# A second order for the first chunk of an attention and softplus-FFN kernel: 582 tasks re-sorted over five engines, 66 of them on another engine

## The chip, the core and the metric

The kernel runs on one core of a Trainium2 chip. The core has a matrix engine (TensorE, PE in the profile), a vector engine (VectorE, DVE), an activation engine (ScalarE, ACT), a general engine (GpSimd, POOL) and a sync engine (SyncE, SP) that here only issues transfers. The metric is the device time of one execution in microseconds (us); lower is better.

## What is computed

Eight batches, eight heads, 576 positions, head width 64. Four heads attend to the last 32 positions, four to the positions at the same place in every 32. Then each token's 512 numbers go through a 512 to 2048 product, a softplus, and a 2048 to 512 product.

```python
scores = scale * np.matmul(q, k.transpose(0, 1, 3, 2))
scores = np.where(masks[None, :, :, :], scores, -1000000000.0)
attn = np.exp(scores - np.max(scores, axis=-1, keepdims=True))
attn = attn / (np.sum(attn, axis=-1, keepdims=True) + 1e-09)
x = np.matmul(attn, v).transpose(0, 2, 1, 3).reshape(B * S, H * D)   # 4608 x 512
h = x @ w_in                                                          # 512 x 2048, float64 weights
g = np.maximum(h, 0.0) + np.log1p(np.exp(-np.abs(h)))
out = g @ w_out                                                       # 2048 x 512, float64 weights
```

## The kernel before, in words

Work is cut twice. Attention goes by *queries* n = 0 to 31, each one batch and one pair of heads; four queries make a batch. The FFN goes by *chunks* of 512 tokens, nine in all, and each chunk by 16 *blocks* f of 128 hidden units. For a block, `hidden` (line 648, 12 matmuls of 512 columns, three for each of four pairs) makes `ph`; ScalarE takes |h|, exp and log (lines 660, 663, 665); VectorE joins them into the softplus `u` (line 669); `u` is split into a high and a low part `gh` and `gl` (lines 264 and 681); `output` (line 688, 12 matmuls) adds the block's share to the four `py` banks. `ph` has two buffers, so block f+2 in the order waits for the softplus of block f.

During the first chunk everything else happens besides: the first eight queries are worked, and all 32 blocks of weights arrive as 64-bit floats (`load_weights`, lines 569 and 575) and are turned into two 32-bit parts each by six steps: `w_abs` (line 589, ScalarE), `w_shift` (line 593), `w_last` (line 602), `w_sign` (line 619, all three VectorE), `w_high` (line 264, a cast) and `w_low` (line 634, a subtraction). A query has its own steps: load q, lay q out (line 264, letter D), load k, scores (S, line 355), maxima (X, line 389), bias (x, line 393) or subtraction, exponentials (E), row sums' guard and reciprocal (r, line 439, and R, line 443), normalising (M, line 447), transposes (T and C on TensorE and a copier for queries 0 to 3; P, line 457, 16 VectorE transposes for queries 4 to 7), the weighted sum (V, line 525) and the two parts of x (H, line 563, and L, line 561).

The order of this first part is not computed. It is the string `FIRST`, a list of task names that is gone through from left to right; each task issues its instructions on its engine's queue, and each engine works its queue strictly in order. A name is a letter for the step and a number for the query or block: `S40` is the first half of the scores of query 4, `F3` the hidden product of block 3, `O3` its output product, `li3` the low part of the input weights of block 3. `Fa0` is the first nine matmuls of block 0 and `F0` the last three; `Q..` are the same steps for the first two blocks of chunk 1. Three further lists, `ON_POOL`, `ON_VECTOR` and `ON_SCALAR`, name the tasks that run on another engine than their usual one: GpSimd's usual tasks are the low parts (`li`, `lo`, `Gl`) and M, VectorE's are r and x, ScalarE's are D, C and the casts (`hi`, `ho`, `Gh`).

Loads are issued on SP's queue, also in order. A load of a query waits there for the buffer that it overwrites (`prob`, `v_in`, `kT`), and everything behind it waits too. The results of chunk 0 (`y0` to `y3`, line 704) are stored from the same queue.

After `FIRST`, a planner (`Plan`) orders the rest from costs and due times. Its first step is the scores of query 8, `S8`, which needs `k8`, the last task but a few of `FIRST`.

Of the kernel before, what the change touches and what calls it, by code (L numbers as in the profile page):

```python
# [33 lines left out]


FIRST = """
q0 D00 k0 W mask D01 S01 q1 X01 x01 D11 q2 D10 S00 X00 Y00 E01 D20 E00 Z00 r0 D21 R0 M0 k1 S10 X10
S11 wi2 ai2 X11 Y11 E11 T00 wi4 k2 S20 ai4 Bi2 x10 E10 di2 k3 ci2 Bi4 Z11 hi2 di4 r1 ci4 T01 C01
C00 q3 D30 D31 T02 X20 R1 Y20 M1 v0 V00 C02 H00 wi1 E20 ai1 S21 X21 L00 Z20 T10 wi0 li2 x21 T11
hi4 Bi1 di1 ci1 E21 r2 V01 H01 L01 C11 wo0 S31 C10 R2 v1 hi1 S30 X30 wo14 li4 wo1 T12 Y30 ai0 X31  # L40
M2 V10 H10 L10 T21 k4 C12 Bi0 v2 wi3 x31 E30 di0 Z30 V11 C21 E31 H11 T20 C20 li1 L11 ao1 T22 r3 R3
M3 V20 T32 ao0 ci0 C22 Bo0 H20 L20 C32 hi0 ai3 T30 C30 do0 wo3 li0 T31 V21 v3 co0 C31 V31 H21 L21
ho0 V30 Bi3 di3 ao3 H30 Fa0 Bo3 ci3 hi3 H31 L30 wi10 q4 D4 L31 F0 lo0 A0 Fa1 do3 co3 li3 Ae0 ho3
Al0 Bo1 do1 u0 S40 X40 wo4 ao4 lo3 Bo4 wo2 ao2 x40 Bo2 Gh0 Gl0 wi8 ai8 wo9 wi6 Bi8 E40 F1 F3 A3
Ae3 do2 di8 ci8 hi8 Al3 co2 do4 co1 ho1 wo5 A1 Ae1 Al1 u3 li8 Gh3 O0 lo1 ho2 lo2 ai6 u1 wi5 ai5
S41 wi11 X41 x41 Gl3 Bi5 Gh1 Gl1 ai11 Bi11 Bi6 E41 F4 wo7 q5 D5 wi9 wi15 F2 A2 di5 O1 di11 Ae2 Al2
di6 ci5 r4 hi5 ci6 wi14 R4 wi12 ci11 hi11 k5 wi13 u2 Gh2 M4 S50 X50 F8 co4 x50 P4 Gl2 O2 li11 A4
Ae4 hi6 ho4 li5 li6 Al4 u4 E50 S51 X51 v4 V40 ai9 Bi9 di9 x51 A8 wo6 Ae8 Al8 wi7 k6 q6 lo4 wo11
ao5 Bo5 O3 ci9 ai7 Bi7 di7 u8 Gh4 Gl4 F5 H40 L40 E51 ci7 ai10 Bi10 r5 R5 F6 Gh8 do5 D6 S60 hi7
di10 Gl8 co5 M5 V41 ci10 A5 Ae5 Al5 u5 O4 li7 A6 Ae6 Al6 X60 x60 u6 ho5 P5 Gh5 Gl5 hi9 lo5 wo12  # L50
li9 F7 H41 hi10 ao7 li10 v5 O5 ao6 Bo6 do6 L41 co6 E60 S61 X61 Gh6 Gl6 A7 Ae7 Al7 x61 Bo7 k7 V50
u7 F9 ho6 lo6 O6 wo10 H50 L50 ai13 Bi13 wo8 ao8 E61 q7 V51 Bo8 D7 di13 do7 A9 Ae9 ci13 r6 R6 hi13
S70 do8 li13 F13 co8 H51 co7 M6 Al9 u9 Gh7 ao10 X70 x70 L51 ho8 Gl7 F10 P6 ho7 ai12 lo7 Gh9 Gl9
lo8 E70 Bi12 Bo10 O7 ao9 Bo9 do10 S71 v6 V60 do9 k9 O8 co9 ho9 A13 Ae13 Al13 u13 F11 di12 A10 Ae10
Al10 Gh13 X71 u10 ao11 Bo11 co10 ho10 lo9 lo10 Gh10 Gl10 x71 H60 L60 do11 ai14 Bi14 O9 A11 V61
ci12 di14 E71 r7 R7 O10 hi12 ai15 ci14 Ae11 li12 H61 L61 co11 hi14 M7 li14 wo15 Al11 u11 F12 P7
Gh11 Gl11 wo13 ao12 A12 Ae12 F14 ho11 lo11 Gl13 ao13 Al12 u12 Gh12 A14 Ae14 Bo12 do12 Gl12 co12
ho12 O11 Bi15 di15 lo12 ci15 ao15 Bo15 v7 V70 H70 L70 ao14 Bo14 Qa0 Al14 u14 O12 q8 D8 hi15 li15
Bo13 do13 co13 ho13 lo13 do14 co14 ho14 V71 H71 F15 A15 Ae15 L71 O13 Q0 Gh14 Gl14 lo14 O14 Al15
u15 Gh15 Gl15 Q1 v8 do15 co15 ho15 lo15 QA0 Qu0 QA1 O15 y0 Qh0 k8 Ob15 Ql0 y3 y2 Qu1 Qh1 Ql1 y1 q9  # L60
"""

ON_POOL = """
x01 D10 D20 hi2 D30 hi0 hi3 ho1 x50 hi6 Gh8 x60 hi13 x70 ho9 Gh13 x71 ho11 hi15 ho14 Gh15 ho15
""".split()
ON_VECTOR = """
D00 M1 C21 M3 li0 lo0 li3 Gl0 li8 Gh3 lo1 Gl3 Gl1 lo4 Gl8 M5 Gl6 li13 lo9 lo10 Gl10 li12 M7 Gl12
lo12 li15 lo13 Gh14 Gl14 lo14 Gl15 lo15
""".split()
ON_SCALAR = """  # L70
y3
""".split()

WIDE = """
# [945 lines left out]
```

## Time and profile before

| | us |
|---|---|
| median of 3 runs | 899.62 |
| lowest and highest run | 898.74, 899.64 |
| the profiled execution's own time | 898.62 |
| its span, first to last instruction | 896.8 |
| TensorE busy in the span | 878.9 |
| VectorE, ScalarE, GpSimd busy | 601.3, 446.8, 58.1 |

The span leaves out 1.8 us of the execution (898.62 less 896.8). TensorE is busy in 98% of the span, so at most 17.9 us can be won by closing its gaps; the matmuls themselves are the same before and after. TensorE's granted clock is 0.999 in this profile. In the views below, a row of the timeline gives start, duration, engine and line, and in brackets the idle time ahead of it with what ended it; a row of the groups gives count, busy time and the mean duration in ns; a row of the stretches gives busy time of PE, PEld (weight loads), DVE, ACT and POOL in turn.

### The profile page before, as it was taken

The numbers are of one execution on the slowest core, as the hardware profiler recorded it, in microseconds if no ns is written. First come the engines' busy times: TensorE is split into PE (matmuls) and PEld (weight loads), VectorE is DVE, ScalarE is ACT, GpSimd is POOL, SyncE is SP. The second block draws the span as 40 slices with busy tenths as digits, with TensorE's granted clock in tenths as the row PEclk, the third lists the DMA queues.
The fourth block names the chain that finished last, engine by engine and source line by source line (L and its number), as shares of the span: only waits on it lengthen the run. The fifth ranks groups of instructions, "written<-read, shape, count | busy, mean of one in ns | idle before, by whom it ended". The sixth has DMA issues, their size and how long they took to land.

```text
span 896.8 us, 14347 instructions
## 1 busy us (share of the span) xinstructions
PE 878.9 (98%) x5632; PEld 722.0 (81%) x5632; DVE 601.3 (67%) x1313; ACT 446.8 (50%) x795; POOL 58.1 (6%) x81
## 2 busy tenths in 40 slices
PE   6899999999999999999999999999999999999998
PEld 4777777888888888888888888888888888888886
DVE  8999996877777677666766676776776333333332
ACT  7998765445444545544544444454443343333332
POOL 6244330000000000000000000000000000000000
PEclk9999999999999999999999999999999999999999
DMA  9882212112211112111211121111200010001001
GB/s 339 297 303 92 86 37 88 44 57 60 76 43 45 44 44 89 32 44 45 91 44 44 42 76 31 44 45 44 91 18 18 1 48 1 0 1 48 1 1 47
DMA packets 50083, 58.27 MB, mean 65 GB/s; under 512 B 3168, under 2 KB 35296, under 8 KB 50016
## 3 DMA queue, kind: packets, MB, share of 16 engines
q1 hardware_dynamic: 49728, 57.03, 19.5%
q8 instruction: 44, 0.72, 0.3%
q10 hardware_dynamic: 288, 0.33, 0.1%
q14 instruction: 23, 0.19, 0.1%
HBM read 47.91 MB, written 9.44 MB: 64 GB/s over the span
## 4 chain that ended last, share of the span: by engine, by line
PE 87%; DVE 8%; ACT 2%; issue 1%; POOL 1%; DMA 0%; SPq 0%; DVEq 0%; POOLq 0%; ACTq 0%
PE py L688 41%; PE ph L648 40%; PE ps L355 2%; PE pv L525 2%; DVE pt L457 2%; PE po L525 1%; PE po L355 1%; DVE a_i L602 1%; DVE a_i L619 1%; DVE a_i L593 1%; DVE u L669 1%; DVE a_o L602 1%; DVE st L389 1%; DVE a_o L619 0%; DMA kT<-in_qk_dram 0%
## 5 line engine op out<-in xcount | busy, mean ns | idle before, releaser
L688 PE MATMUL py<-w_o,gh 128*128 128x512 f32 x1152 | 359.2, 393 | 0.3 <-POOL w_o L634 0.2
L648 PE MATMUL ph<-x_h,w_i 128*128 128x512 f32 x1152 | 356.4, 391 | 1.3 <-DVE w_i L634 0.9
L660 ACT ACTIVATE u<-ph 128x512 f32<-128x512 f32 x144 | 86.2, 599 | 396.8 <-PE ph L648 394.7
L648 PEld LDWEIGHTS ph<-x_h,w_i 128*128 128x128 f32 x1152 | 215.6, 188 | 47.2 <-DVE w_i L634 1.2
L688 PEld LDWEIGHTS py<-w_o,gh 128*128 128x128 f32 x1152 | 214.1, 188 | 47.7 <-POOL w_o L634 1.1
L648 PE MATMUL ph<-x_l,w_i 128*128 128x512 f32 x576 | 224.4, 390 | 0.0
L688 PE MATMUL py<-w_o,gl 128*128 128x512 f32 x576 | 224.4, 390 | 0.0
L669 DVE SCALAR_TENSOR_TENSOR u<-ph,u 128x512 f32<-128x512 f32 x144 | 99.2, 689 | 169.5 <-ACT u L665 167.9
L457 DVE STREAM_TRANSPOSE pt<-prob 32x192 f32<-32x192 f32 x448 | 137.1, 314 | 6.4
L688 PEld LDWEIGHTS py<-w_o,gl 128*128 128x128 f32 x576 | 108.2, 188 | 22.6
L648 PEld LDWEIGHTS ph<-x_l,w_i 128*128 128x128 f32 x576 | 108.2, 188 | 22.5
L681 DVE TENSOR_TENSOR gl<-u,gh 128x512 fp32r<-128x512 f32 x137 | 94.8, 692 | 12.0 <-POOL gh L264 0.8
L663 ACT ACTIVATE u<-u 128x512 f32<-128x512 f32 x144 | 91.2, 633 | 4.5
L665 ACT ACTIVATE u<-u 128x512 f32<-128x512 f32 x144 | 91.0, 632 | 4.3
L264 ACT COPY qT<-prob 64x576 f32<-64x576 f32 x56 | 70.6, 1261 | 2.3 <-DMA prob<-in_qk_dram 1.9
L264 DVE CAST gh<-u 128x512 fp32r<-128x512 f32 x130 | 55.7, 428 | 10.6 <-DVE u L669 0.5
L416 DVE TENSOR_TENSOR prob<-ps,mask_b 128x384 f32<-128x384 f32 x24 | 13.4, 558 | 50.2 <-PE ps L355 50.2
L355 PEld LDWEIGHTS ps<-kT,qT 128*64 128x64 f32 x720 | 24.0, 138 | 9.6 <-issue 8.1
L355 PE MATMUL ps<-kT,qT 128*64 128x64 f32 x720 | 27.6, 225 | 0.9 <-DMA kT<-in_qk_dram 0.9
L525 PE MATMUL pv<-pt,v_in 128*64 128x96 f32 x396 | 22.1, 248 | 1.0 <-PE ps L355 1.0
L447 DVE TENSOR_TENSOR prob<-prob,st 128x576 f32<-128x576 f32 x27 | 21.6, 799 | 0.9
L416 DVE TENSOR_TENSOR prob<-po,mask_b 128x192 f32<-128x192 f32 x24 | 8.6, 357 | 19.3 <-ACT x_h L563 19.3
(101 smaller groups left out, 511.9 us busy)
## 6 DMA issues: line engine op xcount, KB each, us to landing
v_in<-in_v_dram SPq DMA_DIRECT2D x28, 320.0 KB, 3.5
out_dram<-o SPq DMA_DIRECT2D x35, 256.0 KB, 2.1
ri<-in_moe_w_in_dram SPq DMA_DIRECT2D x16, 512.0 KB, 8.0
ro<-in_moe_w_out_dram SPq DMA_DIRECT2D x16, 512.0 KB, 6.9
kT<-in_qk_dram SPq DMA_DIRECT2D x28, 288.0 KB, 2.9
prob<-in_qk_dram SPq DMA_DIRECT2D x28, 288.0 KB, 2.7
v_in<-in_v_dram SPq DMA_DIRECT2D x28, 48.0 KB, 2.7
room<-in_v_dram SPq DMA_DIRECT2D x4, 320.0 KB, 6.8
```

Of the source, the lines that this page charges most:

```text
L264: (engine.copy if engine is nc.scalar else engine.tensor_copy)(dst, src)
L355: nc.tensor.matmul(ps[rows[place], 64 * (x - lo) : 64 * (x - lo) + 64], lhsT=blocks_of(n)[:, c // 32].rearrange("p h l -> p (h l)"), rhs=k ...
L416: nc.vector.tensor_tensor(pv, sv, m, op=ALU.add)
L457: nc.vector.transpose(pt[32 * (i + c) : 32 * (i + c) + 32, h, a : a + hi - lo, 32 * i : 32 * i + 32,], src[:, lo:hi, 32 * c : 32 * c + 32],)
L525: nc.tensor.matmul(po[64 * h : 64 * h + 64, TILE * x : TILE * x + TILE], lhsT=vs[n][:, a, h, :], rhs=pt_of(n, a)[:, h, a % 2], start=True, ...
L648: nc.tensor.matmul(ph, lhsT=w32["i", f][:, half, cc * P : (cc + 1) * P], rhs=x_of(x, cc)[:, t0 : t0 + n], start=(i == 0), stop=(i == 3 * N ...
L660: nc.scalar.activation(us[c, f], phs[c, f], AF.Abs)
L663: nc.scalar.activation(u, u, AF.Exp, scale=-1.0)
L665: nc.scalar.activation(u, u, AF.Ln, bias=1.0)
L669: nc.vector.scalar_tensor_tensor(u, in0=phs.pop((c, f)), scalar=0.0, in1=u, op0=ALU.max, op1=ALU.add)
L681: engine.tensor_tensor(g, us.pop((c, f)), ghs[c, f].bitcast(F32), op=ALU.subtract)
L688: nc.tensor.matmul(py[t], lhsT=g[:, sl], rhs=w32["o", f][:, half], start=(f == 0 and n == 0), stop=(f == NFC - 1 and n == 2),)
```

## The change

`FIRST` is replaced by another list of the same names; no task is added or dropped, and `Plan` is not touched. Of the three engine lists, `ON_POOL` grows from 22 names to 36, `ON_VECTOR` goes from 32 to 31, `ON_SCALAR` keeps one name (`y1` for `y3`). The table, cut to its first lines and its end:

```diff
 FIRST = """
-q0 D00 k0 W mask D01 S01 q1 X01 x01 D11 q2 D10 S00 X00 Y00 E01 D20 E00 Z00 r0 D21 R0 M0 k1 S10 X10
+W mask q0 D01 D00 k0 S01 q1 D10 D11 k1 S00 X01 x01 E01 S11 X00 Y00 X11 Y11 E00 q2 D20 Z00 S10 X10
...
-Bo13 do13 co13 ho13 lo13 do14 co14 ho14 V71 H71 F15 A15 Ae15 L71 O13 Q0 Gh14 Gl14 lo14 O14 Al15
-u15 Gh15 Gl15 Q1 v8 do15 co15 ho15 lo15 QA0 Qu0 QA1 O15 y0 Qh0 k8 Ob15 Ql0 y3 y2 Qu1 Qh1 Ql1 y1 q9
+ho15 u15 Gh15 Gl15 O14 lo15 Qu0 Qh0 Ql0 Q1 QA1 Ob15 Qu1 O15 k8 y1 y0 y2 Qh1 Ql1 y3
 """
 
 ON_POOL = """
-x01 D10 D20 hi2 D30 hi0 hi3 ho1 x50 hi6 Gh8 x60 hi13 x70 ho9 Gh13 x71 ho11 hi15 ho14 Gh15 ho15
+D11 x01 D20 r0 x10 hi1 x21 r1 hi8 x31 r3 hi2 hi6 hi5 hi3 x41 ho1 r4 x50 ho3 x51 r5 x60 ho7 hi7 Gh8
+r6 Gh10 x71 hi14 r7 Gh13 ho12 hi15 ho14 ho15
 """.split()
 ON_VECTOR = """
-D00 M1 C21 M3 li0 lo0 li3 Gl0 li8 Gh3 lo1 Gl3 Gl1 lo4 Gl8 M5 Gl6 li13 lo9 lo10 Gl10 li12 M7 Gl12
-lo12 li15 lo13 Gh14 Gl14 lo14 Gl15 lo15
+D00 M0 li1 M3 C22 li6 Gh0 Gl0 li5 li3 lo1 Gl2 Gh5 Gl5 li9 Gl9 lo5 Gl6 lo6 Gl8 M6 li12 lo10 li14
+li15 Gl13 Gh14 Gl14 lo14 Gh15 lo15
 """.split()
```

Counted over these lists, GpSimd gains 4 biases (x), 7 guards (r), 4 casts, one weight low part, one `Gl` and one M, and loses one D. VectorE loses those biases and guards, one low part, one `Gl` and one M, and gains two casts of `Gh`: its queue has 12 rows fewer. ScalarE loses casts and gains one D. Line numbers after the edit are one higher throughout, since the string has one line more.

**GpSimd at the start.** The rows that follow the last clearing memset; `st` is the small table of maxima, sums and reciprocals of a query, `raw_q` a loaded q, `early_l` and `early_h` the buffers of queries 0 to 3. Before:

```order
L393 TENSOR_SCALAR st_0_175<-st_0_175 128x3
L264 COPY early_h2_92<-raw_q1_173 64x18x32
L264 COPY early_h1_94<-raw_q2_179 64x18x32
L447 TENSOR_TENSOR early_l0_91<-early_l0_91,st_0_175 128x9x64
L264 CAST w_i_2_283<-a_i_2_235 128x512
L264 COPY early_h3_96<-raw_q3_301 64x18x32
L634 TENSOR_TENSOR w_i_2_283<-a_i_2_235,w_i_2_283 128x512
```

And now, from the same place:

```order
L265 COPY early_h2_92<-raw_q1_173 64x32x18
L394 TENSOR_SCALAR st_0_192<-st_0_192 128x3
L265 COPY early_h1_94<-raw_q2_212 64x18x32
L440 TENSOR_SCALAR st_0_192<-st_0_192 128x9
L394 TENSOR_SCALAR st_1_208<-st_1_208 128x6
L265 CAST w_i_1_265<-a_i_1_236 128x512
L394 TENSOR_SCALAR st_2_275<-st_2_275 128x3
L440 TENSOR_SCALAR st_1_208<-st_1_208 128x9
L448 TENSOR_TENSOR early_l2_93<-early_l2_93,st_1_208 128x9x64
```

The first bias (`x01`, the `128x3` row) now stands behind a copy of q, the guards have come in from VectorE, and the first normalising (`M0`) has gone to VectorE, with that of query 1 (`M1`) here in its place.

**TensorE at the first blocks.** `ph_0_0` and `ph_0_1` are blocks 0 and 1, `ps_4_0` the scores `S40` of query 4 with their mask. From the last matmuls of block 0, before:

```order
L648 MATMUL ph_0_0_617<-x_l3_632,w_i_0_551 128x512
L648 MATMUL ph_0_1_646<-x_h0_331,w_i_1_409 128x512 x2
L648 MATMUL ph_0_1_646<-x_l0_347,w_i_1_409 128x512
L648 MATMUL ph_0_1_646<-x_h2_455,w_i_1_409 128x512 x2
L648 MATMUL ph_0_1_646<-x_l2_457,w_i_1_409 128x512
L648 MATMUL ph_0_1_646<-x_h1_546,w_i_1_409 128x512 x2
L648 MATMUL ph_0_1_646<-x_l1_548,w_i_1_409 128x512
L340 LDWEIGHTS ident_b_108
L340 MATMUL ps_4_0_666<-mask_b_89,ident_b_108 64x384
```

Now:

```order
L649 MATMUL ph_0_0_625<-x_l3_617,w_i_0_507 128x512
L341 LDWEIGHTS ident_b_108
L341 MATMUL ps_4_0_654<-mask_b_89,ident_b_108 64x384
L341 LDWEIGHTS ident_b_108
L341 MATMUL ps_4_0_654<-mask_b_89,ident_b_108 64x384
L356 MATMUL ps_4_0_654<-kT_0_100,qT_99 64x64 x12
L649 MATMUL ph_0_1_685<-x_h0_331,w_i_1_265 128x512 x2
```

The scores of query 4 now stand directly behind block 0; the nine matmuls of `Fa1` that lay between come after them.

**SP at the end of the chunk.** `v_in` is the load of `v8`, `kT_0` that of `k8`, `out_0_dram` the stores of chunk 0. Before:

```order
L293 DMA v_in_102<-in_v_dram 96x128
L300 DMA v_in_102<-in_v_dram 128x5x128
L704 DMA out_0_dram<-o_0_0_1778 128x512
L282 DMA kT_0_100<-in_qk_dram 128x576
L704 DMA out_0_dram<-o_0_3_1792 128x512
```

Now:

```order
L294 DMA v_in_102<-in_v_dram 96x128
L301 DMA v_in_102<-in_v_dram 128x5x128
L283 DMA kT_0_100<-in_qk_dram 128x576
L705 DMA out_0_dram<-o_0_1_1791 128x512
L705 DMA out_0_dram<-o_0_0_1794 128x512
```

The load of `k8` has moved past the first store, ahead of all four.

More of the change, by code (lines that the diff above doesn't have):

```diff
@@ L36 @@
 FIRST = """
-q0 D00 k0 W mask D01 S01 q1 X01 x01 D11 q2 D10 S00 X00 Y00 E01 D20 E00 Z00 r0 D21 R0 M0 k1 S10 X10
[L38 to L58, printed above, removed]
-Bo13 do13 co13 ho13 lo13 do14 co14 ho14 V71 H71 F15 A15 Ae15 L71 O13 Q0 Gh14 Gl14 lo14 O14 Al15
@@ L60 @@
-u15 Gh15 Gl15 Q1 v8 do15 co15 ho15 lo15 QA0 Qu0 QA1 O15 y0 Qh0 k8 Ob15 Ql0 y3 y2 Qu1 Qh1 Ql1 y1 q9
+W mask q0 D01 D00 k0 S01 q1 D10 D11 k1 S00 X01 x01 E01 S11 X00 Y00 X11 Y11 E00 q2 D20 Z00 S10 X10
+D21 wi1 k2 r0 ai1 x10 E10 R0 M0 T01 Bi1 di1 ci1 E11 Z11 wi8 hi1 S21 X21 x21 wo0 T00 ai8 Bi8 di8
+C01 ao0 Bo0 r1 R1 do0 C00 q3 D31 S20 X20 M1 v0 V00 H00 k3 T02 C02 D30 L00 V01 T10 ci8 hi8 li1 E21
+Y20 E20 co0 S31 li8 X31 x31 wi0 Z20 wi2 v1 H01 L01 r2 v3 T11 C11 S30 R2 T12 X30 Y30 M2 C10 ai0 Bi0
+ho0 lo0 V10 H10 L10 T20 C12 V11 E30 Z30 E31 r3 di0 wi6 H11 C20 ai2 T21 L11 C21 R3 ci0 hi0 wi3 ai3
@@ new lines @@
+M3 li0 Bi2 T22 v2 V20 H20 C22 L20 T32 C32 di2 T31 ci2 ai6 Bi6 T30 C31 C30 V21 H21 L21 V31 wi5 ai5
+wo7 di6 ci6 V30 Bi3 H30 H31 L31 wo9 q4 D4 di3 Fa0 L30 F0 k4 hi2 Bi5 di5 hi6 li6 A0 Ae0 Al0 wo1 ci5
+S40 X40 x40 E40 k5 wi4 ai4 hi5 Fa1 F1 u0 S41 li2 A1 Gh0 Gl0 O0 ci3 q5 ao1 li5 Ae1 Al1 hi3 D5 Bo1
+li3 F3 X41 wo3 wo5 Bi4 di4 do1 co1 x41 E41 S50 ci4 ho1 ao3 u1 Bo3 wo2 do3 r4 R4 M4 v4 wi11 co3 X50
+x50 wi14 A3 Ae3 Al3 ao7 u3 wo4 Bo7 Gh1 Gl1 Gh3 hi4 E50 lo1 F2 P4 A2 Ae2 Gl3 ao2 Al2 u2 li4 F5 A5
+Ae5 Al5 O1 ho3 lo3 V40 k6 Bo2 do2 co2 S51 Gh2 Gl2 u5 ho2 H40 L40 lo2 X51 F4 wi9 F6 ao4 Bo4 ai9 Bi9
@@ new lines @@
+do4 di9 ci9 A4 wo15 Gh5 wi15 Gl5 q6 co4 O2 ai11 Bi11 x51 do7 co7 D6 hi9 li9 E51 S60 r5 R5 M5 Ae4
+Al4 A6 di11 ho4 X60 x60 V41 H41 L41 wi10 ai10 u4 P5 v5 ho7 Gh4 E60 Ae6 Al6 Bi10 Gl4 lo4 O3 F9 ci11
+A9 O4 V50 ao5 Bo5 do5 wi7 u6 Ae9 Al9 k7 hi11 lo7 u9 li11 ai7 wi13 S61 F8 Gh6 Gh9 Bi7 wo13 di7 co5
+H50 wo6 F11 wo14 Gl9 di10 ho5 lo5 O5 ao6 Bo6 do6 wo8 ci7 co6 A8 Ae8 Al8 ai13 hi7 li7 X61 x61 Bi13
+u8 Gh8 L50 ho6 q7 D7 Gl6 F7 lo6 O6 E61 S70 di13 Gl8 ci13 ao8 Bo8 do8 V51 r6 A7 Ae7 co8 hi13 Al7
+A11 u7 ao9 R6 M6 Bo9 do9 Ae11 wo10 li13 F13 v6 Gh7 Gl7 O7 H51 L51 X70 Al11 u11 wi12 ci10 hi10 li10
@@ new lines @@
+ho8 F10 co9 ho9 lo9 lo8 wo11 O8 x70 P6 V60 Gh11 Gl11 ao10 Bo10 ai12 Bi12 di12 A13 do10 E70 S71
+ci12 A10 co10 Ae10 Al10 O9 ai14 H60 Ae13 Al13 wo12 u10 Gh10 L60 u13 hi12 V61 li12 F12 Bi14 ho10
+ao11 Bo11 Gl10 q8 D8 lo10 X71 ao12 di14 ci14 x71 H61 v7 Bo12 do12 k9 E71 A12 Ae12 do11 Al12 hi14
+li14 co11 r7 R7 u12 Gh12 O10 F14 L61 co12 ho11 M7 P7 Qa0 lo11 O11 ai15 Bi15 ao13 Bo13 Gl12 ao14
+A14 Ae14 di15 ci15 Al14 V70 q9 Gh13 ho12 lo12 O12 u14 H70 L70 hi15 li15 V71 H71 v8 do13 co13 ho13
+Gl13 L71 F15 ao15 Gh14 A15 Bo14 do14 co14 Ae15 Al15 Gl14 lo13 O13 Q0 QA0 ho14 lo14 Bo15 do15 co15
@@ L69 @@
+li15 Gl13 Gh14 Gl14 lo14 Gh15 lo15
 """.split()
 ON_SCALAR = """
-y3
+y1
 """.split()
```

## The prediction

> **What bounds the kernel now.** The page's busy shares (TensorE 98%) say only that gaps of TensorE are what can be won. So I read its busy time by stretch, then the chain of waits in order of time, and last the groups of VectorE and GpSimd in the stretch that the change touches.
>
> ```profile
> 0.00:32.60 32.60, 22.00 (x480) 17.02 (x480) 28.20 (x60) 25.45 (x68) 18.40 (x42) 1.00 0.87 304
> 32.60:55.00 22.40, 22.40 (x154) 17.81 (x150) 22.04 (x45) 22.01 (x50) 5.03 (x5) 1.00 1.05 369
> 55.00:119.00 64.00, 61.56 (x395) 48.43 (x395) 62.84 (x141) 52.01 (x131) 30.77 (x31) 1.00 0.34 114
> 119.00:145.40 26.40, 26.32 (x131) 20.77 (x131) 21.92 (x40) 15.38 (x25) 3.87 (x6) 1.00 0.12 35
> ```
>
> TensorE idles 10.6 us before its first FFN product (32.60 less 22.00), nothing to 55 us, 2.4 us to 119 and 0.1 to 145.4, where 0.9 more lie in front of one instruction (below). So outside the start some 3.4 us are to be had. From 55 to 119 us VectorE is busy 62.84 of 64.00 us. The chain says that it is what TensorE waits for:
>
> ```profile
> 32.72 5.00 PE ph L648 x21
> ...
> 54.55 0.69 DVE u L669
> ...
> 117.74 1.30 POOL w_o L634
> ...
> 142.91 3.46 DMA kT<-in_qk_dram
> ```
>
> Up to 32 us most links are VectorE's; from 32.72 the matmuls carry it for a while; from the softplus at 54.55 it is VectorE again, to a hand-over through GpSimd at 119; then the matmuls, but for one transfer at 142.91. The change can therefore act in three places: the length of the start, VectorE's pace up to 119 us, and that transfer. I take the TensorE work itself as unchanged.
>
> **The transfer (a gain, quite sure).** The scores of query 8 wait for their k:
>
> ```profile
> 146.41 0.92 PE L355 MATMUL ps<-kT,qT 128*64 128x64 f32 x24 [0.94 <-DMA kT<-in_qk_dram]
> ```
> ```profile
> 128.25 0.39 SPq L300 DMA_DIRECT2D v_in<-in_v_dram  x1
> 142.50 0.35 SPq L704 DMA_DIRECT2D out_dram<-o  x1
> 142.91 0.42 SPq L282 DMA_DIRECT2D kT<-in_qk_dram  x1
> ```
>
> SP had nothing to issue from 128.64 (128.25 plus 0.39) to 142.50: it waited for the first result's copy, and k8 stood behind that store. Now k8 stands directly behind the load of v8. Its buffer was last read by query 6, so it goes out near 128.7 and, at the 3.46 us that it took, lands near 132, over 14 us before it is needed. All of the 0.94 us goes; next in line is the block in front, which TensorE runs without a gap. **-0.9 us**, between -0.94 and 0.
>
> **The start (32.6 us).** The first chain gets longer by a copy:
>
> ```profile
> 7.06 0.23 POOL L393 TENSOR_SCALAR st<-st 128x3 f32<-128x3 f32 x1
> 7.25 2.44 POOL L264 COPY early_h<-raw_q 64x576 f32<-64x576 f32 x2
> 10.12 1.15 POOL L447 TENSOR_TENSOR early_l<-early_l,st 128x576 f32<-128x576 f32 x1 [0.44 <-ACT early_h L264]
> ```
>
> x01 ran at 7.06, as soon as GpSimd was free; now it follows a copy of 1.22 us (half of 2.44). That pushes query 0's exponentials, its sums and its guard by some 1.2 us. M0, 1.15 us on GpSimd, is now on VectorE, where the same work on another query took 0.76 (row below), so the first transposes come about 0.5 us later (11.8 for 11.3). Meanwhile VectorE does query 1's maxima, which it used to do after. Counting its queue from there to the last x_l before block 0: 59 rows before, 54 now; three guards and three biases fewer (0.1 us each by their starts), one w_last more (0.6): level. What differs is what stands late. Walking the rows by hand at the old durations, the first x_l of the second pair comes at the old time, 23.7 us; from there 19 rows and 8.8 us remain where there were 22 and 9.3. **-0.5 us.** As bounds: the walk leaves out collisions with GpSimd beyond the old ones. The old start lost 1.1 us to each of the two worst (rows below), so without those it would be -2.5; two more of them give +1.7.
>
> Right behind block 0 stands S40, which needs q4 laid out by ScalarE:
>
> ```profile
> 33.40 2.56 ACT L264 COPY qT<-prob 64x576 f32<-64x576 f32 x2
> ```
>
> The layout ends at 35.96. In the chain above, 21 matmuls took 5.00 us from 32.72: the twelve of block 0 end near 35.6, and until now nine of block 1 covered the rest. With that cover gone TensorE waits up to 0.4 us; if the layout also comes earlier, nothing. **+0.3 us** (0 to +0.7).
>
> **VectorE's pace (54.6 to 119 us).** VectorE has 12 rows fewer and GpSimd 17 more. Their sizes, and what they cost each other, over 10 to 140 us:
>
> ```profile
> L619 DVE SCALAR_TENSOR_TENSOR a_i<-ri,a_i 128x512 uint32<-128x512 uint32 x16 | 12.3, 768 | 0.1
> L602 DVE SCALAR_TENSOR_TENSOR a_i<-ri,a_i 128x512 uint32<-128x512 uint32 x16 | 12.2, 772 | 0.2
> L602 DVE SCALAR_TENSOR_TENSOR a_o<-ro,a_o 128x512 uint32<-128x512 uint32 x16 | 11.2, 708 | 0.1
> L619 DVE SCALAR_TENSOR_TENSOR a_o<-ro,a_o 128x512 uint32<-128x512 uint32 x16 | 10.9, 685 | 0.2
> L593 DVE TENSOR_SCALAR a_i<-a_i 128x512 uint32<-128x512 uint32 x16 | 8.7, 548 | 0.0
> L593 DVE TENSOR_SCALAR a_o<-a_o 128x512 uint32<-128x512 uint32 x16 | 6.7, 422 | 0.0
> L634 DVE TENSOR_TENSOR w_o<-a_o,w_o 128x512 fp32r<-128x512 f32 x9 | 6.2, 686 | 1.5 <-POOL w_o L264 0.7 <-ACT w_o L264 0.7
> L634 DVE TENSOR_TENSOR w_i<-a_i,w_i 128x512 fp32r<-128x512 f32 x6 | 5.1, 844 | 0.0
> L447 DVE TENSOR_TENSOR prob<-prob,st 128x576 f32<-128x576 f32 x3 | 3.4, 1120 | 0.0
> L393 DVE TENSOR_SCALAR st<-st 128x3 f32<-128x3 f32 x5 | 2.2, 445 | 0.0
> L439 DVE TENSOR_SCALAR st<-st 128x9 f32<-128x9 f32 x7 | 2.2, 316 | 0.0
> L264 DVE CAST gh<-u 128x512 fp32r<-128x512 f32 x3 | 1.6, 528 | 0.1
> L447 DVE TENSOR_TENSOR early_l<-early_l,st 128x576 f32<-128x576 f32 x1 | 0.8, 761 | 0.0
> L393 DVE TENSOR_SCALAR st<-st 128x6 f32<-128x6 f32 x2 | 0.3, 162 | 0.0
> ```
> ```profile
> L634 POOL TENSOR_TENSOR w_o<-a_o,w_o 128x512 fp32r<-128x512 f32 x7 | 9.4, 1336 | 7.9 <-ACT w_o L264 7.8
> L264 POOL CAST w_i<-a_i 128x512 fp32r<-128x512 f32 x6 | 3.9, 655 | 19.3 <-DVE a_i L619 9.4 <-ACT x_h L563 4.1 <-DVE st L439 3.9
> L393 POOL TENSOR_SCALAR st<-st 128x6 f32<-128x6 f32 x3 | 1.1, 366 | 7.5 <-DVE st L389 7.5
> ```
> ```profile
> 10.00:140.00 130.00, 120.33 (x1048) 96.23 (x1044) 125.59 (x266) 104.85 (x252) 49.28 (x47) 1.00 0.51 178
> ```
>
> The same instruction of the same size is longer in one group than in its twin. A row that was hit shows why, with GpSimd's beside it:
>
> ```profile
> 18.87 0.15 DVE L393 TENSOR_SCALAR st<-st 128x3 f32<-128x3 f32 x1
> 18.94 1.51 DVE L593 TENSOR_SCALAR a_i<-a_i 128x512 uint32<-128x512 uint32 x1
> ```
> ```profile
> 18.88 1.28 POOL L634 TENSOR_TENSOR w_i<-a_i,w_i 128x512 fp32r<-128x512 f32 x1 [1.65 <-ACT w_i L264]
> ```
>
> A 0.42 us row took 1.51: it ended 0.3 us after GpSimd's did. Summed as mean less twin times count: w_shift 16 x 0.126 = 2.0; w_sign 16 x 0.083 = 1.3; w_last 16 x 0.064 = 1.0; w_low 6 x 0.158 = 0.9; M 3 x 0.359 = 1.1; biases 5 x 0.283 = 1.4; guards 7 x 0.154 = 1.1 (against the six-column row's 162, the nearest). That is 8.8 us of VectorE's time for 49.3 of GpSimd's, 18%.
>
> VectorE sheds one w_low, one `Gl` (taken like it), one M and 11 short rows, and takes two casts: 0.69 + 0.69 + 0.76 + 11 x 0.16 - 2 x 0.53 = 2.8 us by durations. Rows overlap by 0.07 or so (18.87 to 18.94 above for a row of 0.15), so I take 2.1. GpSimd gains 1.34 + 1.34 + 1.15 (low part, `Gl` taken like it, M at 10.12), 4 x 0.66 of casts, at most 11 x 0.37 of short rows, and sheds a copy of 1.22: 9.3, or 7.8 with the short rows at 0.23 (the 7.06 row); I take 8.4. At 18% that costs VectorE 1.5. Net -0.6 us of work on the path, and I pass it to TensorE as it is. It can't bring more than the 2.4 us of idle time there; if all 8.4 us blocked, it would cost 6.3. **-0.6 us** (-2.4 to +6.3).
>
> The Trainium skill's rule speaks against this edit: the page "SBUF — State Buffer", section "Who interferes with whom", makes VectorE and GpSimd share one port pair as an exclusive lock, so that a VectorE instruction with two SBUF inputs, or a copy, cast or tensor_scalar in a two-port mode, blocks for the whole of a GpSimd instruction that started first. The 1.51 us row agrees. Read at its worst, every added GpSimd instruction meets such a row, and the sum would be 6.9 us worse than mine; read as issue order decides, the 18% stands.
>
> **Weights ahead of queries.** No row in which TensorE waits for a weight transfer exists before, so bringing some forward is worth nothing by itself. The other side costs nothing either as long as the late blocks land in time, which I take them to do.
>
> **The sum.** -0.9 - 0.5 + 0.3 - 0.6 = -1.7 us. The profiled execution took 898.62, so it would read 896.9; the median lies 1.0 above it, so I predict 899.62 - 1.7 = 897.9. A measurement of this kernel tells about 0.2% apart, 1.8 us, so the line to "faster" runs at 897.8 and that to "slower" at 901.4.
>
> **The rivals.**
> 1. *The sum holds* (897.9; its own range 896.3 to 899.3). Chance 0.40, half of it beyond the line.
> 2. *The order feeds TensorE better than VectorE's load says.* Softplus rows unblock `ph`. Counting rows in VectorE's queue, the 5th stands at row 99 and before at row 113, the 11th at 163 for 184, the 15th at 212 for 226. If the gaps between 55 and 119 us close, all 2.4 go in place of 0.6: 896.1. Against it: the 7th softplus stands behind the same transposes of a query, at row 131 for 135 with more VectorE time ahead. Chance 0.25.
> 3. *GpSimd becomes VectorE's brake.* The point from which it decides: when over 2.1 / 8.4 = 25% of the added time blocks, the third term turns positive. At 75%, with moved steps meeting w_last and w_sign rows directly, it is +4.2 in place of -0.6, and with the start at +0.5 for the same reason: 903.7; at 50%, with the start as in the sum, it is 900.6. For it: 18% is an average over a GpSimd that idles more. Against: the guards and biases that were hit worst are no longer VectorE's. Chance 0.20, three quarters of it over 901.4.
> 4. *The change doesn't pay:* one stall replaces another, in the start and in the middle (each at 0 or a little above), and only the transfer's 0.9 is left: 898.7 to 900. Chance 0.15.
>
> Faster: 0.20 + 0.22 = 0.42. Slower: 0.15 and a little of case 4, 0.18. The same: 0.40. The range takes in case 2 with a start that is 1 us better, 895.2, and half of case 3's spread, 902.2.
>
> **What would show it.** In the new profile S8 should start without a wait for kT, with k8 issued near 129 us: if it waits, the first term falls. The first FFN product should start within a microsecond of 32.6: if it is over 34, the start was the cost. A wait in front of S40 for ScalarE's copy up to 0.7 us. TensorE's idle time from there to 119 us should be near 1.8 instead of 2.4, GpSimd's busy time near 66.5, VectorE's rows in the groups with means near those above; if w_last and w_sign rise over 0.85, case 3 is at work. Any TensorE wait for a weight's transfer would make the last paragraph on the loads wrong.

## The result, and the profile after

The changed kernel takes 893.80 us (median of 4 runs, 893.55 to 894.77) against 899.63 for the kernel before (4 runs): a ratio of 0.994, 95% interval 0.9922 to 0.9957. That is 5.8 us, where 1.7 were forecast, and below the range. The profiled execution took 893.55 us, with a span of 891.6.

From the start of the scores of query 8 (S8) to the end of the last matmul it is 746.57 us in both traces. All of the gain lies ahead of S8, which starts at 141.22 in place of 146.41. TensorE by stretch, columns as in the prediction:

```profile
0.00:32.60 32.60, 26.23 (x487) 21.28 (x488) 26.88 (x58) 27.01 (x71) 21.31 (x49) 0.95 0.92 311
32.60:55.00 22.40, 21.82 (x159) 17.19 (x159) 21.50 (x47) 21.40 (x57) 12.32 (x13) 1.00 0.85 308
55.00:119.00 64.00, 63.56 (x405) 51.62 (x400) 61.94 (x138) 54.87 (x123) 31.45 (x32) 1.00 0.39 132
119.00:145.40 26.40, 26.40 (x164) 21.15 (x163) 21.56 (x37) 13.06 (x21) 5.42 (x6) 1.00 0.26 89
10.00:140.00 130.00, 124.57 (x1072) 101.94 (x1068) 122.92 (x261) 106.84 (x255) 61.70 (x64) 0.99 0.53 182
```

From 32.6 to 145.4 us TensorE stands still for 1.0 us (0.58 + 0.44), before for 2.5 (2.4 + 0.1) and another 0.94 in front of S8. The rows that mark the parts, from TensorE's timeline (the first FFN product, S40 with its mask, the two waits left over 0.2 us, and S8):

```profile
31.03 0.73 PE L649 MATMUL ph<-x_h,w_i 128*128 128x512 f32 x2
...
33.98 0.35 PE L341 MATMUL ps<-mask_b,ident_b 128*64 128x384 bf16 x2
...
38.77 0.27 PE L341 MATMUL ps<-mask_b,ident_b 128*64 128x192 bf16 x2 [0.54 <-ACT prob L400]
...
75.46 0.73 PE L649 MATMUL ph<-x_h,w_i 128*128 128x512 f32 x2 [0.29 <-DVE u L670]
...
141.22 0.92 PE L356 MATMUL ps<-kT,qT 128*64 128x64 f32 x24
```

The first FFN product starts 1.6 us earlier; before, it was

```profile
32.64 0.73 PE L648 MATMUL ph<-x_h,w_i 128*128 128x512 f32 x2
```

From there to S8 it is 110.19 us in place of 113.77: 0.94 of the difference is the transfer, 2.6 the middle. So 5.2 = 1.6 + 0.9 + 2.6 by the trace; the two profiled executions are 5.1 apart. Of the 2.6, only 1.5 is idle time (2.5 less 1.0). The other 1.1 is TensorE's busy time, 110.3 us before and 109.2 now for the same 676 matmuls. It goes with the waits: in the two runs below that take the waits away in the old order, it is 109.0 and 109.3.

The groups of VectorE that the prediction rested on, 10 to 140 us:

```profile
L603 DVE SCALAR_TENSOR_TENSOR a_i<-ri,a_i 128x512 uint32<-128x512 uint32 x16 | 11.1, 694 | 0.2
L620 DVE SCALAR_TENSOR_TENSOR a_i<-ri,a_i 128x512 uint32<-128x512 uint32 x16 | 10.9, 683 | 0.2
L594 DVE TENSOR_SCALAR a_i<-a_i 128x512 uint32<-128x512 uint32 x16 | 7.0, 434 | 0.1
L635 DVE TENSOR_TENSOR w_i<-a_i,w_i 128x512 fp32r<-128x512 f32 x8 | 5.9, 741 | 0.0
L265 DVE CAST gh<-u 128x512 fp32r<-128x512 f32 x6 | 4.5, 743 | 0.3
```

GpSimd is busier (61.70 us for 49.28), and yet, for the input weights, w_last fell from a mean of 772 ns to 694, w_sign from 768 to 683, w_shift from 548 to 434. The casts of `gh` rose most (528 to 743). To have one number for all kernels below, I call *VectorE's loss* the time that its rows took beyond the usual time of their kind undisturbed, summed row by row from 0 to 146 us with differences over 0.05 us counted. The kinds and their usual times are 0.42 us for w_shift, 0.69 for w_last, w_sign and the low parts (`Gl` too), 0.76 for M, 0.16 to 0.17 for biases and guards, 0.43 for the casts of `gh`. The loss is 10.2 us before and 4.6 after. GpSimd's rows show where the rest of the waiting went:

```profile
L682 POOL TENSOR_TENSOR gl<-u,gh 128x512 fp32r<-128x512 f32 x8 | 11.5, 1437 | 2.1 <-ACT gh L265 1.5 <-PE py L689 0.5
L265 POOL CAST w_i<-a_i 128x512 fp32r<-128x512 f32 x9 | 7.0, 782 | 19.7 <-DVE a_i L620 6.7 <-ACT u L666 5.3 <-ACT early_l L382 2.5
```

The same cast took 655 ns before. GpSimd is now 4.0 us busier than the forecast's 57.7 (49.3 + 8.4). Measured like VectorE's loss (usual: the shortest tenth of the rows of a kind), GpSimd's rows lose 8.7 us where they lost 4.2: VectorE waits 5.6 us less, GpSimd 4.5 more. One cast undisturbed and one that met VectorE, and the VectorE row that it met:

```profile
36.09 0.62 POOL L265 CAST w_i<-a_i 128x512 fp32r<-128x512 f32 x1 [3.63 <-DVE a_i L620]
...
39.65 1.01 POOL L265 CAST w_i<-a_i 128x512 fp32r<-128x512 f32 x1 [1.68 <-DVE a_i L620]
```
```profile
39.51 0.68 DVE L635 TENSOR_TENSOR w_i<-a_i,w_i 128x512 fp32r<-128x512 f32 x1
```

VectorE's row started 0.14 us ahead, kept its usual 0.68 us, and the cast ran 0.4 us long. In the pair that the prediction shows GpSimd was 0.06 us ahead, and VectorE's row took 1.51 us for 0.42. This agrees with the Trainium skill's page "SBUF — State Buffer", section "Who interferes with whom": whoever issues first holds the port pair, and the other waits.

The traces show it through the whole stretch. Every VectorE row that lost time, 16 before and 13 after, began inside a GpSimd row, and it lost what was left of that row less 0.12 to 0.15 us (the pair in the prediction: 1.23 us left, 1.09 lost). With 0.2 us or less left, it lost nothing; two rows after lost nothing with 0.46 us left, beside a GpSimd row that had itself been held up. So what counts is how early in a GpSimd row a VectorE row starts. Before, eight rows started early enough to lose 0.8 to 1.1 us each, 8.3 of the 10.2; after, one did. The size of the damage is set by the order in time, not by how much GpSimd does.

### The profile page after: what moved, and what is told of

It is laid out like the page before. It is cut to its first block, busy times and chain, and to the rows that moved or that the text cites. A ratio compares the mean times of both kernels' runs of the same rounds, so it can differ in the third digit from the quotient of the medians.

```text
span 891.6 us, 14349 instructions
## 1 busy us (share of the span) xinstructions
PE 880.4 (99%) x5632; PEld 725.3 (81%) x5632; DVE 594.8 (67%) x1301; ACT 444.4 (50%) x790; POOL 70.5 (8%) x98
## 4 chain that ended last, share of the span: by engine, by line
PE 91%; DVE 4%; ACT 3%; POOL 1%; issue 0%; POOLq 0%; DVEq 0%; ACTq 0%
PE py L689 43%; PE ph L649 42%; PE ps L356 2%; PE pv L526 2%; PE po L526 1%; DVE pt L458 1%; PE po L356 1%; ACT early_h L265 0%; DVE a_i L603 0%; ACT prob L400 0%; ACT early_l L400 0%; ACT a_i L590 0%; DVE a_i L620 0%; DVE a_o L603 0%; ACT qT L265 0%
## 5 line engine op out<-in xcount | busy, mean ns | idle before, releaser
L265 ACT COPY qT<-prob 64x576 f32<-64x576 f32 x56 | 70.5, 1260 | 0.3
L265 DVE CAST gh<-u 128x512 fp32r<-128x512 f32 x132 | 58.1, 440 | 10.3
L564 ACT CAST x_h<-pv 128x288 fp32r<-128x288 f32 (+2 forms) x47 | 16.6, 369 | 10.0 <-PE pv L526 9.9
```

Of the source, the lines that this page charges most:

```text
L265: (engine.copy if engine is nc.scalar else engine.tensor_copy)(dst, src)
```

## The experiments

Theory: the start and the middle were won because VectorE lost less beside GpSimd (and had 2.1 us fewer of its own); rival: the new order feeds TensorE better, or gets GpSimd's results earlier, and the shorter rows are a symptom. Each kernel was timed in 5 rounds beside the kernel before (898.9 to 899.6 us in these). The "first FFN" and "S8" columns are starts in the profiled execution.

| kernel | us | ratio, 95% interval | first FFN | S8 | VectorE's loss |
|---|---|---|---|---|---|
| before | 899.63 | | 32.64 | 146.41 | 10.2 |
| after | 893.80 | 0.9922–0.9957 | 31.03 | 141.22 | 4.6 |
| order alone | 926.39 | 1.0286–1.0315 | 36.85 | 174.91 | 17.6 |
| lists alone | 921.52 | 1.0233–1.0261 | 34.69 | 170.03 | 17.2 |
| before, k8 early | 898.59 | 0.9985–1.0002 | 33.42 | 146.50 | 9.9 |
| before, short rows on GpSimd | 898.82 | 0.9986–1.0004 | 32.81 | 146.42 | 8.8 |
| after, S40 back | 895.97 | 0.9944–0.9969 | 31.03 | 143.58 | 3.8 |
| after, x01 first | 893.73 | 0.9924–0.9951 | 30.99 | 141.27 | 4.5 |
| after, guards back | 894.17 | 0.9930–0.9955 | 31.38 | 141.85 | 4.4 |
| after, weights of block 15 late | 896.15 | 0.9952–0.9977 | 31.05 | 142.79 | 3.6 |
| after, S41 later | 894.51 | 0.9938–0.9962 | 31.09 | 142.14 | 4.5 |
| after, k8 back | 897.57 | 0.9972–0.9991 | 31.03 | 144.04 | 4.6 |
| before, GpSimd cut short | 894.63 | 0.9940–0.9965 | 31.59 | 141.89 | 3.7 |
| after, GpSimd cut short | 893.57 | 0.9928–0.9953 | 31.93 | 142.06 | 1.0 |
| after, low parts twice | 915.71 | 1.0171–1.0199 | 34.37 | 162.80 | 19.4 |
| after, more on VectorE | 901.74 | 1.0018–1.0039 | 33.43 | 148.53 | 6.3 |
| before, less on VectorE | 896.25 | 0.9948–0.9974 | 32.35 | 142.91 | 8.1 |

In the three kernels that are over 10 us slower, the first chunk runs on past 146 us; counted up to S8, their losses are 18.5, 20.0 and 20.7, in the order of the table.

**The halves of the change.** First the new `FIRST` with the three old engine lists, then the old `FIRST` with the three new ones; the lines are those of "The change" above.

> The new list, with the three engine lists of before. Theory 'order': the 5.8 us come from the list itself, which makes VectorE's rows and GpSimd's instructions miss each other (VectorE lost 10.2 us to rows that ran longer than their twins before, 4.6 after) and feeds TensorE in time; then this kernel keeps most of it, 893.8 to 895.8. Rival 'lists': the steps taken off VectorE make the gain; then this kernel stands near 897 to 899, with only the 0.9 us of the transfer of k8 and a little more left. Both expect k8 to land in time.

> The old list, with the three new engine lists. 'Order': GpSimd's extra 8 us meet VectorE's rows as they fall, so no gain and perhaps a loss, 899 to 902. 'Lists': 895 to 896.5, the gain less the transfer's 0.9.

Both missed by a wide margin: either half alone makes the kernel 22 to 27 us slower. The longest waits of TensorE in the first and then in the second, by what was waited for (us in total, times, longest):

```profile
PE ps L340 <- ACT prob L399: 5.0, 2, 3.6
PE py L688 <- DVE w_o L634: 3.8, 3, 1.6
```
```profile
PE ph L649 <- DVE u L670: 6.2, 5, 2.4
PE py L689 <- DVE gh L265: 3.5, 1, 3.5
PE py L689 <- DVE gl L682: 3.3, 1, 3.3
```

With 66 tasks on another engine than the order was made for, results come late on queues that are worked strictly in order; that is how I read these waits. Order and engines are one design, and no sum over the two halves exists. What they do show: the lists do not set VectorE's loss (17.2 with the new lists in the old order, 4.6 in the new), nor does the order alone (17.6 with the old lists).

**GpSimd cut short.** In the kernel before and in the changed one, in place. The lines below cut the low parts of the weights to 128 of 512 columns; `Gl` is cut likewise and M to two of nine places, and TensorE reads the part that is there in place of the rest. So these kernels leave out most of those results:

```diff
+        a, n = part.pop((w, f)).bitcast(F32), DM
+        if engine is nc.gpsimd:
+            cut_w.add((w, f))
+            n = P
         engine.tensor_tensor(
-            t[:, 1], part.pop((w, f)).bitcast(F32), t[:, 0].bitcast(F32), op=ALU.subtract
+            t[:, 1, :n], a[:, :n], t[:, 0, :n].bitcast(F32), op=ALU.subtract
         )
```

> The kernel before with GpSimd's long steps cut short and nothing moved: where GpSimd takes a low part of weights (17 times), a low part of activations (7) or a normalisation (4), it works on 128 of 512 columns, or 2 of 9 heads' places, and TensorE reads the columns that are there, so that every matmul, wait and place in a row stays. What it leaves out: three quarters of those low parts and normalisations. GpSimd's busy time from 10 to 140 us should fall from 49.3 to about 20 us. Theory (the gain of the change came from fewer collisions of VectorE with GpSimd: 10.2 us lost in the rows of before, 4.6 in after, and 4.2 us of the gain in start and middle): the loss falls to about 4.4 us and the time by 4 us, to 894.5-896.5 us. Rival (the new order feeds TensorE better and the longer rows are only a symptom): 898.5-899.8.

> The changed kernel with the same cut of GpSimd's low parts and normalisations (the same work left out). Theory (collisions): only 4.6 us are lost there and TensorE stands still for 1.3 us, so that at most 1 us is left to win: 892.5-893.8. Rival (GpSimd's results come earlier, and that alone is what the cut brings): as much as in the kernel before, 3 to 4 us, so 890-891.

The theory held in both. The kernel before fell to 894.63, 4.2 us under the 898.86 of the kernel timed beside it, with no task moved; the changed kernel did not gain (893.57). GpSimd's time fell less than expected (to 26.76 us for about 20), the loss a little more (to 3.7 for 4.4). The kernel before with the cut, over two stretches, and the two rows that are in the prediction with 0.15 and 1.51 us:

```profile
55.00:119.00 64.00, 63.81 (x421) 51.32 (x420) 62.68 (x150) 53.76 (x134) 15.04 (x30) 1.00 0.30 102
...
10.00:140.00 130.00, 123.26 (x1074) 100.48 (x1069) 123.33 (x274) 108.95 (x259) 26.76 (x47) 1.00 0.51 180
```
```profile
19.58 0.15 DVE L393 TENSOR_SCALAR st<-st 128x3 f32<-128x3 f32 x1
19.64 0.42 DVE L596 TENSOR_SCALAR a_i<-a_i 128x512 uint32<-128x512 uint32 x1
```

TensorE's 2.4 us of idle time from 55 to 119 us are 0.2 in the old order. From the first FFN product to S8 it is 110.30 us, of which 0.79 are still the wait for k8, so 109.5, no more than the 110.19 of the new order. The old order feeds TensorE as well as the new one, once VectorE isn't held. In the cut version of the changed kernel VectorE loses another 3.6 us less and the same stretch takes 110.13: there is nothing left to win there. Its start was 0.9 us later in the profiled execution, the slowest of its five (894.50). The granted clock in the first 32.6 us was 0.90 there for the 0.95 above, but that is not shown to be the reason: with weights late and with S41 later it was 1.00, and the first FFN product started no sooner (31.05 and 31.09).

**VectorE's own time.** Shorter steps of GpSimd also end earlier. So eight w_last steps were left out in the kernel before (the last three bits of those blocks' weights are then zero), and eight (not the same ones) taken twice in the changed one, with GpSimd as it was:

```diff
         if engine is nc.vector:
+            if f"{w}{f}" in "i2 i4 i1 i5 i11 i6 i9 i7".split():
+                return
```
```diff
+            for _ in range(2 if f"{w}{f}" in "i1 i8 o0 o2 o4 i9 o7 i11".split() else 1):
+                engine.scalar_tensor_tensor(
```

> The kernel before with 8 of VectorE's steps on the weights' last bits left out (the last three bits of those blocks' weights are then zero), 3 at 11 to 21 us, 5 at 50 to 67 us: 4.8 us less of VectorE's time, GpSimd's row as it is. Theory (VectorE's time goes through by 0.65 to 1): 894.0-896.0. Rival (GpSimd's late results, not VectorE's time): 898.5-899.6.

> The changed kernel with 8 of VectorE's steps on the weights' last bits taken twice (the second writes the same bits): 3 of them at 12 to 17 us, 5 at 55 to 66 us. At the pitch of 0.605 us that is 4.8 us more of VectorE's time; GpSimd's row is as it is. Theory (VectorE's time goes through to the end, by 0.65 to 1 of it, as 6.5 us fewer lost gave 4.2 us with GpSimd's steps cut): 896.9-898.6. Rival (VectorE's time has cover, and GpSimd's earlier results were the gain): 893.5-894.5.

Less on VectorE: 896.25, a quarter of a microsecond outside the theory's range and over 2 from the rival's. S8 comes 3.5 us earlier for 4.8 us of steps and 2.1 of loss fewer. With GpSimd's work untouched, TensorE's idle time closes as well:

```profile
55.00:119.00 64.00, 63.78 (x418) 51.00 (x418) 62.77 (x145) 53.19 (x133) 32.27 (x30) 1.00 0.32 108
```

More on VectorE: 901.74, 7.9 us for 4.8, more than the theory allowed. The nine times spread from 900.59 to 903.71, the longest at a mean granted clock of 0.992 to 0.994, so the trace is the better measure: S8 comes 7.3 us later. The loss rose by 1.7 too (4.6 to 6.3), and TensorE met a long wait:

```profile
74.97 0.73 PE L650 MATMUL ph<-x_h,w_i 128*128 128x512 f32 x2 [2.21 <-DVE u L671]
```

So VectorE's time is the path. In the old kernel, half to two thirds of what is taken away reaches S8 (3.5 of 6.9 us here, 4.5 of 6.5 with GpSimd cut short); in the new one, more than what is added does (7.3 for 6.5).

**More on GpSimd.** Each low part of weights on GpSimd taken twice, in the changed kernel:

```diff
+        for _ in range(2 if engine is nc.gpsimd else 1):
+            engine.tensor_tensor(t[:, 1], a, t[:, 0].bitcast(F32), op=ALU.subtract)
```

> The changed kernel with each low part of weights on GpSimd taken twice (18 more instructions of 1.3 us, the same result written again): GpSimd's busy time rises by some 24 us. Theory (collisions): VectorE loses between 7% (4.6 us of 62) and 18% (before) of that, 1.7 to 4.3 us, so 895-898. Rival (GpSimd stands still for more than half of the time, and what it does there is free while its results are not late): 893.5-894.5.

915.71, 22 us slower, far above both. VectorE's loss rose by 14.8 us (4.6 to 19.4), and TensorE waited for GpSimd itself:

```profile
PE py L689 <- POOL w_o L637: 5.2, 4, 2.4
PE ph L649 <- POOL w_i L637: 3.8, 3, 1.7
```

So this run mixes two causes. It does show that GpSimd's idle time (61.70 busy of 130) is no room to work in: neither 7% nor 18% is a price.

**The short rows.** In the kernel before, five biases and seven guards to GpSimd; in the changed one, the guards back to VectorE (`ON_POOL`, each line cut to its start; `r4` to `r7` leave the list likewise in the second):

```diff
-x01 D10 D20 hi2
+x01 x10 x21 x31 x41 x51 r0 r1 r3 r4 r5 r6 r7 D10 D20 hi2
```
```diff
-D11 x01 D20 r0 x10 hi1 x21 r1 hi8 x31 r3 hi2
+D11 x01 D20 x10 hi1 x21 hi8 x31 hi2
```

> Before, with only the short rows moved to GpSimd: 5 biases (x10, x21, x31, x41, x51) and 7 guards (r0, r1, r3 to r7). They lost 2.5 us of VectorE's time to GpSimd before. 'Lists': 897 to 898.5. 'Order': 899 to 901, since the row behind them is hit in their place and each step now crosses to GpSimd and back.

> The changed kernel, with all eight guards (r) back on VectorE. Guards lost 1.1 us of VectorE's time to GpSimd before. Theory 'the short rows off VectorE make the difference': 894.5 to 895.5. Rival 'they don't': 893.5 to 894, VectorE has time to spare now.

898.82 and 894.17: neither is to be told from the kernel that it started from. Which engine takes the short rows is not what was won.

**The transfer of k8.** Moved alone in the kernel before, and moved back behind the first store in the changed one (each line cut to the place):

```diff
-v8 do15
+v8 k8 do15
...
-y0 Qh0 k8 Ob15
+y0 Qh0 Ob15
```
```diff
-O15 k8 y1 y0 y2
+O15 y1 k8 y0 y2
```

> Before, with one name moved: k8 directly behind v8. All theories: the 0.94 us wait of the scores of query 8 goes and nothing takes its place, 898.5 to 898.8. If the wait of TensorE goes and the time stays at 899.6, the term was not worth its size.

> The changed kernel with the load of query 8's keys back behind the first result's transfer in SP's queue. Theory (the scores of query 8 then wait for the keys as before, 0.94 us, and nothing lies behind that could take it up): 894.5-894.9. Rival (that load has cover): 893.5-894.1.

Alone it gave 0.57 us, with an interval that takes in no change: the wait was gone in its trace, but its first FFN product stood 0.8 us later. Moved back it cost 3.8 us, four times the theory. Its twelve times run from 896.11 us at a mean granted clock of 0.997 to 900.21 at 0.992, so the clock is part of that price. SP's timeline and TensorE's, and the clock (after the comma PE, PEld, DVE, ACT, POOL; then the granted clock):

```profile
139.32 0.35 SPq L705 DMA_DIRECT2D out_dram<-o  x1
139.72 0.42 SPq L283 DMA_DIRECT2D kT<-in_qk_dram  x1
```
```profile
144.04 0.92 PE L356 MATMUL ps<-kT,qT 128*64 128x64 f32 x24 [2.65 <-DMA kT<-in_qk_dram]
```
```profile
131.00:141.00 10.00, 10.00 (x46) 8.26 (x44) 7.21 (x12) 4.81 (x9) 2.23 (x2) 1.00 0.09 28
144.00:148.80 4.80, 4.76 (x45) 3.98 (x46) 3.73 (x7) 3.17 (x3) 0.00 (x0) 0.64 0.29 89
```

In the new order TensorE is ready for S8 4.1 us earlier (141.39 for 145.47, each start less its wait), the first store is issued only 3.2 earlier (139.32 for 142.50), and the transfer behind it takes 4.3 us to land for 3.5. So the wait grows by 0.9 and by 0.8, to 2.65 us. And TensorE then runs at a granted clock of 0.64 on the mean of some 5 us, 0.50 from 145.3 to 148.6: from S8 to the end it is 748.19 us instead of 746.57, 1.6 more.

**S40, x01, S41.** Three edits of single places in the changed kernel's order (each line cut to the place; with S40, `ai4` stays behind `E40`):

```diff
-S40 X40 x40 E40 k5 wi4 ai4 hi5 Fa1 F1
+k5 wi4 hi5 Fa1 S40 X40 x40 E40 ai4 F1
```
```diff
-q1 D10 D11 k1 S00 X01 x01 E01
+q1 D10 k1 S00 X01 x01 D11 E01
```
```diff
-u0 S41 li2 A1 Gh0 Gl0 O0 ci3
+u0 li2 A1 Gh0 Gl0 O0 S41 ci3
```

> The changed kernel, with the scores S40 put back behind the nine matmuls of Fa1 (and the weight step ai4 kept behind E40). S40 did not wait in the changed kernel, so the cover of Fa1 is worth nothing there: theory 'no cover needed' 893.8. Rival: S41 already waits 0.54 us for the exponentials of S40; with S40 2.2 us later that wait grows to some 2 us and the time to 895 to 896.

> The changed kernel, with the bias x01 ahead of the copy D11 on GpSimd. From 8.70 to 27.8 us ScalarE ran without a pause and its first link waited 1.55 us for that bias. Theory 'ScalarE's chain sets the start': it begins near 7.3, and the time falls by 0.7 to 1.2, to 892.6 to 893.1. Rival: the scores of query 1 come 0.25 us later behind D11, ScalarE waits there, and nothing is won: 893.6 to 894.

> The changed kernel with the second scores of query 4 (S41) one place later, behind block 0's output products: the wait of 0.54 us for the exponentials of the first half is covered. Theory (a wait of TensorE counts in full): 893.1-893.5. Rival (the maxima and exponentials that follow S41 come 1.3 us later and the next products wait for them): 893.8-895.5.

The rival was right in all three. S40 behind the nine matmuls costs 2.2 us: the second half of query 4's scores then waits longer for the exponentials of the first, and the clock falls again. From the first FFN product to S8 TensorE stands still for 1.1 us more and is busy for 1.2 more:

```profile
40.01 0.27 PE L341 MATMUL ps<-mask_b,ident_b 128*64 128x192 bf16 x2 [1.99 <-ACT prob L400]
```
```profile
40.00:45.60 5.60, 5.59 (x29) 4.56 (x29) 4.86 (x10) 5.54 (x10) 1.50 (x3) 0.70 1.07 386
```

x01 ahead of the copy wins nothing. S41 one place later moves its wait of 0.54 us to the next scores, and costs 0.7 us; TensorE's row there:

```profile
45.87 0.35 PE L341 MATMUL ps<-mask_b,ident_b 128*64 128x384 bf16 x2 [0.73 <-ACT prob L400]
```

**Weights ahead of queries.** The two loads of block 15 moved from ahead of q6 to behind v6 (each line cut to the place):

```diff
-A4 wo15 Gh5 wi15 Gl5 q6
+A4 Gh5 Gl5 q6
...
-F13 v6 Gh7
+F13 v6 wo15 wi15 Gh7
```

> The changed kernel, with the loads of the two blocks wo15 and wi15 moved back from ahead of q6 to behind v6. They are used some 30 us after they then land, so 893.8 by the theory that loads ahead of queries are worth nothing; 894.5 or more if q6 or v6, or the steps on these blocks, wait for it.

It cost 2.4 us, and not because block 15 came late. On SP's queue its two loads now stand between v6 and `wi12`, the input weights of block 12, which land at 99.27 us for 96.38. ScalarE's, VectorE's and TensorE's timelines, in this order:

```profile
99.35 0.68 ACT L590 ACTIVATE a_i<-ri 128x512 f32<-128x512 f32 x1 [1.75 <-DMA ri<-in_moe_w_in_dram]
```
```profile
104.20 0.69 DVE L670 SCALAR_TENSOR_TENSOR u<-ph,u 128x512 f32<-128x512 f32 x1 [1.18 <-ACT u L666]
```
```profile
107.61 0.50 PE L649 MATMUL ph<-x_h,w_i 128*128 128x512 f32 x1 [0.40 <-DVE w_i L635]
```

ScalarE stands still for the weights of block 12, the |h|, exp and log of another block are queued behind that step, VectorE's softplus waits for those, and S8 comes 1.6 us later. No row of TensorE names the transfer.

## Why the prediction was wrong

**The step that failed** is "At 18% that costs VectorE 1.5. Net -0.6": the price of GpSimd's added work. The ratio of VectorE's loss to GpSimd's time was taken from the old trace as if it were a property of the two engines. It is one of the order: 10.2 us beside 49 before, 4.6 beside 62 after, 17 in both halves of the change, 19.4 with the low parts twice. In place of +1.5 the loss moved by -5.6. The forecast did see that the biases and guards would no longer be hit on VectorE, and 2.3 of the 5.6 lie there; but moving those rows alone, in the old order, brought the loss only to 8.8. Together with the 2.1 us that VectorE shed by the prediction's estimate, that is 7.7 us of VectorE's time (its busy time on the page fell by 6.5, from 601.3 to 594.8), and 4.2 of them came out as the start's 1.6 and the middle's 2.6. The bound beside it ("It can't bring more than the 2.4 us of idle time there") was too low as well: 1.1 of the middle's 2.6 are not idle time at all.

That VectorE's time is enough to win this much is shown by the two runs in the old order: with GpSimd cut short, and with fewer steps on VectorE, the same idle time closed without a task moved. That it is what the new order won follows from its lower loss, read in its trace. Why the new order has its rows begin so that GpSimd waits rather than VectorE was seen row by row, but not varied; that part is argued from the traces. Whether the new order would win anything at equal loss can't be tried cleanly, since its halves can't be parted. The nearest is the run with more on VectorE: by steps and loss its VectorE has 1.2 us less to do than the kernel before (-2.1 + 4.8 + 6.3 - 10.2), and it is 2.1 us slower, so nothing there speaks for a gain from the order itself. But its added steps stand in places of their own.

**The transfer** (-0.94): right in mechanism, place and size by the trace (k8 went out at 124.52, for the 129 named), though the timed run of it alone (-0.57) can't be told from nothing. What the sum missed is that the term depends on the others: in an order that reaches S8 earlier, the same move is worth 3.8 us, a part of it the clock's.

**The start** (-0.5, measured -1.6): inside its bounds, and nearer to the bound of -2.5 that it gave "without those" two collisions. VectorE's loss between 10 and 32 us fell from 3.3 to 0.4. The first bias did stand behind the copy of q, and putting it back won nothing.

**S40** (+0.3, measured 0): the layout ended at 34.32, not 35.96, and S40 started at 33.98 without a wait. The forecast saw only the cover that S40 lost. It missed that the earlier S40 lets the exponentials begin sooner, which is worth 2.2 us with what the clock adds.

**Weights ahead** ("worth nothing by itself"): wrong in the new order, where the place of two loads is worth 2.4 us. TensorE's waits were searched for a weight's transfer; ScalarE is the engine that reads the raw weights first, and the load that came late was not one that had moved but one behind them on SP's queue.

**The rivals.** In size the second was nearest (896.1): of the 2.4 us of gaps from 55 to 119 us, 0.4 are left. Its cause, softplus rows further forward in VectorE's queue, was not needed for that. The third had the right mechanism with the wrong sign: GpSimd and VectorE do brake each other, and GpSimd took most of the braking over. Of the signs named, S8 without a wait was seen, and TensorE's idle time up to 119 us is 1.0 (0.58 + 0.44) for the forecast 1.8; the first FFN product lay outside the microsecond given (31.03), GpSimd was busier than forecast (70.5 for 66.5), and w_last and w_sign fell.

## What to carry to other kernels

Before one prices work moved to an engine that shares something with the bound engine, one should look at the rows that were hit and ask which of the two started first: the loss can fall while the load rises. A move's worth belongs to the order that it stands in; the terms of a sum over an order are not independent, and half of a jointly made order can be far worse than either whole. When looking for what a transfer holds up, follow the engine that reads it, what is queued behind that step, and the loads behind the transfer on its own queue, not the bound engine alone.

## What the runs showed of the hardware

A wait of TensorE can cost more than itself. Soon behind the waits of 1.99 us (S40 back) and 2.65 us (k8 back) the granted clock was 0.50 for some 3.3 us (40.3 to 43.6 and 145.3 to 148.6; 0.70 and 0.64 on the mean of the rows shown); the second cost 1.6 us more. With the low parts taken twice, a wait of 1.66 us ahead of 94.94 was followed by the same 0.50 (95.8 to 99.0). But the length does not decide it alone: behind waits of 2.40 us in that same kernel (ahead of 117.30) and of 2.21 us with more on VectorE the clock stayed at 1.00 (117.3 to 122, 75 to 85). Behind the kernel before's wait of 0.94 us nothing was lost (746.57 us from there to the end, as without it). The Trainium skill's page "TensorE: Matmul & The Clock Gate", section "Why this matters for your kernels", warns of idle gaps over about 3 us; here shorter ones were enough at times.

A VectorE row that lost time to GpSimd lost what was left of the GpSimd row when it began, less 0.12 to 0.15 us, in the traces before and after alike.
